# A token fold of 21 products with repeated operands, and row transposes in 128x128 blocks, in a fused attention and Fourier-mix kernel

## The chip, the cores and the metric

The kernel runs on one NeuronCore of a Trainium2 chip. The metric is the device time of one execution in microseconds (us); three executions of the kernel before gave a median of 248.39 us (248.08 to 248.51). The engines are named as in the profile: PE (matrix products; PEld is its weight load), DVE, ACT and POOL (vector, activation and general engines), SP (here a DMA issuer).

## The reference

```python
def reference(q, k, v, n_global, n_local, w_ch1, w_ch2):      # q, k, v: (4, 8, 768, 64) float32
    scores = q @ k.T / sqrt(64) - slope[h] * dist              # kept: causal band of 96, and the first 8 keys
    a = softmax(where(keep, scores, -1e9)) @ v
    x = a.transpose(0, 2, 1, 3).reshape(4, 768, 512)
    u = x + real(fft(fft(x, axis=1), axis=2))                  # over tokens, then over features
    un = (u - mean(u)) / sqrt(var(u) + 1e-6)
    return u + maximum(un @ w_ch1, 0) @ w_ch2                  # w_ch1: 512x2048, w_ch2: 2048x512
```

## The kernel before

The four batches go through four stages. **Attention**: q and k are loaded as fp16 and turned with the head dimension on the partitions (tile `pt`, copied to `qkT`), scores go to PSUM tiles `sc`, ACT takes the exponential (`ex`), and `av` (line 808) multiplies by v (tile `pav`) and normalises on DVE into `x`. In batch 0 and 1 the global keys come in through small copies `kB` and `vB` that POOL or DVE make. **Token fold**: the 768 tokens are six blocks of 128, and the six-point part of the transform over tokens combines them into six sums `z`. In batch 0 two of the four pairs of heads are folded on DVE and two (`PEF = (1, 3)`) on PE, by `fold_pe` (line 1004): each of the six sums is a chain of four or six 128x128 products of a scaled identity (1, -1, 1/2 or -1/2) with one block of `x`, 32 in all, into PSUM tile `pf`; ACT or DVE copies the result to `zy`. **Mix**: units `py` (line 1092; tables `t` over tokens), `px` (line 1156) and `pu` (line 1180; tables over features) add up to the rows `u`. **Feed-forward**: rows are centred into `un`, turned into `unT`, multiplied by the first matrix (`ph`, line 1329, 128 products of 256 columns for a chunk of 256 rows), passed through relu into `hT`, and multiplied by the second one (`pg`, or for later chunks a seven-product scheme with tiles `pgA` and `pgD`).

There are twelve chunks of 256 rows. The first three (`NTD = 3`) are turned by PE in `nt_unit` (line 1296): each of 2 x 4 blocks of 128x128 is cut into four 64x64 quarters, 32 transposes in all, each on its own quarter of the PE array, into the two PSUM banks of tile `ptu`; one copy by DVE (line 1321) or ACT (line 1319) brings it to `unT`. Later chunks are turned by DMA.

The order of work on each engine is a table written by hand, `Plan.ORDER` (line 242), of unit names for PE and of operation names for the others. A cost model of times in the class `Plan` walks that table: it only decides in which sequence the engines' lists are interleaved when the program is recorded, and which of several equal PSUM banks a unit takes. The recorded sequence in turn decides who waits for whom where two engines write parts of one tile.

Of the kernel before, what the change touches and what calls it, by code (L numbers as in the profile page):

```python
# [14 lines left out]
P = 128  # L15
# [9 lines left out]
class Plan:  # L25
# [9 lines left out]
    MIX = 1.3  # L35
    LANDED = {"HW": 0.55, "SW": 1.3}
    LAT = {"ACT": 0.14, "DVE": 0.12, "POOL": 0.08}
# [84 lines left out]
    def op_go(self, eng, name, start):  # L122
# [6 lines left out]
        if eng == "POOL":  # L129
            self.ports.append((start, end, 1 if dma else 0 if outs and outs[0][0] in ("vB", "kB") else 2))  # L130
        if dma:
            at = max(max(end + 0.55, 5.5) if eng == "POOL" else end + lat + 2.7 * (lat == 1.0 and end > 3.5), self.now)
# [19 lines left out]

    SHARED = {"kB": 1, "vB": 1, "sid": 1, "f1": 0, "f2": 0, "f3": 0, "z": 0, "g0": 0, "w": 0, "s": 0, "w2a": 0, "w2t": 0, "ex": 0}
# [3 lines left out]
    def beside(self, start, cost, kind):  # L157
# [4 lines left out]
        if names:  # L162
            s = self.op_start("POOL", names[-1])
            if s is not None:
                p = self.made[names[-1]]
                ports = ports + [(max(s, start), max(s, start) + p[0]["POOL"][0], 1 if p[7] else 0 if p[3] and p[3][0][0] in ("vB", "kB") else 2)]
# [15 lines left out]
    def move(self, go=False):  # L182
# [4 lines left out]
        both = [h[2] for k, h in act if k != "AQ" or sw]  # L187
        each = sum(both) * (self.MIX if len(both) > 1 else 1.0) / 1000.0
        rate = {k: h[2] / 1000.0 if k == "AQ" and not sw else each for k, h in act}
        t = min([self.now + h[1] * rate[k] for k, h in act] + [h[0] for k, h in heads if h[0] > self.now + 1e-9] + [self.NEVER])  # L190
        if not go:
            return t
# [3 lines left out]
        for k, q in self.q.items():  # L196
            if q and q[0][1] <= 1e-4:
                _, _, _, outs, uses, cell = q.pop(0)
                cell[0] = t + (1.3 + 0.4 * (t > 12) if k == "SW" else 1.1 if t < 8 else self.LANDED["HW"] + 0.7)
# [144 lines left out]
def act(n):  # L344
    return 0.1 + n / 1180.0
# [10 lines left out]
def pool(n):  # L356
    return 0.16 + n / 1080.0


@with_exitstack  # L360
def kernel(
# [156 lines left out]
    def load_v(b, hp):  # L518
        h0 = 2 * hp
        if b >= FB:  # L520
# [3 lines left out]
            swq(whole, 1.08, [("avdone", b - 2), ("wl", 7)], [("v", b, hp, t) for t in range(2)], (1536, 0.93), False)  # L524
            return
        if b == 1:
            for t in range(2 - hp % 2 * 2):
# [3 lines left out]
                swq(four, 1.08, [], [("v", b, hp, t), ("v", b, hp + 1, t)], (1536, 0.93))  # L531
            return
        for t in range(2):
# [3 lines left out]
            swq(run, 0.85, ([("avdone", b - 2), ("wl", 7)] if b > 1 else []), [("v", b, hp, t)], (768, 0.93), b < 2)  # L537
# [4 lines left out]
    def load_qk(b, hp):  # L542
# [3 lines left out]
        for w, src in enumerate((q, k)):  # L546
            if b >= FB:
                for h in range(2):
# [4 lines left out]
                    swq(run, 0.85, free(tag, ti) + [("wl", 7)], [("qk", n, w, h)], (768, 0.93), False)  # L553
# [25 lines left out]
            if n == 4:  # L579
# [5 lines left out]
                swq(two, 1.08, free(tag, ti), [("qk", n, w), ("qk", n + 1, w)], (1536, 1.53))  # L585
# [7 lines left out]
            swq(run, 0.85, free(tag, ti), [("qk", n, w)], (768, 1.53))  # L593
# [110 lines left out]
    def score(b, hp, g):  # L704
# [3 lines left out]
        def run(start, ring):  # L708
# [37 lines left out]
            e = pl.pe((0.45, 0.45, 0.34)[g] if pem else 0.24, start, "64x64" if pem else "64x32")  # L746
# [61 lines left out]
    def av(b, hp):  # L808
# [28 lines left out]
        def part(start, ring, x, k):  # L837
# [15 lines left out]
            pl.later([("DVE", 0.17 + 0.03 * m + m * dve(384), lambda: norm(po, k))], free(*XT[b]), e,  # L853
# [10 lines left out]
    def bounce(b):  # L864
# [26 lines left out]
        pl.later([("POOL", 1.1, rg)], xw + [("xr", b), ("c", "back")], 0.0, [("xg", b)], dma=(128, 4.94), rank=0)  # L891

    def fold_s(b):
# [3 lines left out]
        for n, (c0, cw) in enumerate(parts):  # L897
# [43 lines left out]
            pl.later([("DVE", (4 if b else 2) * dve2(cw), f3)], [("f2", b, n)], 0.0, [("f3", b, n)])  # L941
# [8 lines left out]
    def fold_0():  # L950
# [41 lines left out]
        def g0(x):  # L992
            if x == 0:
# [6 lines left out]
        ZS = (((one, 0), (one, 3), (one, 1), (one, 4), (one, 2), (one, 5)), ((one, 0), (neg, 3), (neg, 1), (one, 4), (one, 2), (neg, 5)),  # L1000
              ((one, 0), (one, 3), (mhlf, 1), (mhlf, 4), (mhlf, 2), (mhlf, 5)), ((one, 0), (neg, 3), (half, 1), (mhlf, 4), (mhlf, 2), (half, 5)),
              ((one, 1), (one, 4), (neg, 2), (neg, 5)), ((one, 1), (neg, 4), (one, 2), (neg, 5)))

        def fold_pe(hp):
            cols = slice(hp * P, (hp + 1) * P)

            def run(start, ring):
                zy()
                pf = bank(ring, f"pf_{hp}")
                for n, terms in enumerate(ZS):  # L1010
                    o = pf[:, n // 4, (n % 4) * P:(n % 4 + 1) * P]
                    for x, (w, i) in enumerate(terms):
                        nc.tensor.matmul(o, w, X[0][:, i, cols], start=(x == 0), stop=(x == len(terms) - 1))
# [120 lines left out]
    def mirror(b):  # L1134
# [8 lines left out]
        pl.later([("POOL", 0.8, lambda: r0(nc.gpsimd.tensor_copy)), ("DVE", 0.3, lambda: r0(V.tensor_copy))], [("y", b, 0, 3), ("y", b, 3, 3)] + free("rev0", b), 0.0,  # L1143
# [116 lines left out]
    def centre(c):  # L1260
# [11 lines left out]
        for a in range(2):  # L1272
            pl.later([("ACT", 0.62, lambda a=a: un("ACT", a)), ("DVE", 1.3 if c < 2 else 0.38, lambda a=a: un("DVE", a))],
# [13 lines left out]
        pl.later([("POOL", 0.82, rstd)], [("ss", c, 0), ("ss", c, 1)], 0.0, [("rstd", c)], rank=2)  # L1287
# [8 lines left out]
    def nt_unit(b, pr):  # L1296
# [4 lines left out]
        def run(start, ring):  # L1301
            pt = bank(ring, f"ptu_{c}", FP16)
            un = T.pop(("un", c))
            for a in range(2):
                for d in range(ND):
                    for i in range(2):
                        for h in range(2):
                            r, o, x = slice(64 * i, 64 * i + 64), d * P + 64 * h, 64 * (a * ND + d)
                            nc.tensor.transpose(pt[64 * h:64 * h + 64, i, x:x + 64], un[r, a, o:o + 64], idn[r, r],
                                                tile_position=(64 * i, 64 * h))  # L1310
# [40 lines left out]
    def store_back(c, needs):  # L1351
# [6 lines left out]
        pl.later([("POOL", 1.1, st)], needs, 0.0, [], [("free", "u", c + pl.U0)] * 2, dma=(128, 11.25), rank=0)  # L1358
# [71 lines left out]
    def s_sums(c):  # L1430
# [16 lines left out]
        def s1():  # L1447
            VT(new(0), block(1, 0), block(1, 1), op=ALU.add)

        def s3():  # L1450
            VT(block(1, 0), block(0, 0), block(1, 0), op=ALU.subtract)

        def s2():
            VT(new(1), SX[c, 0], block(0, 0), op=ALU.subtract)

        def s4():
            if lean:
                SX[c, 2] = SX[c, 1]
                VT(SX[c, 2], block(0, 1), SX[c, 1], op=ALU.subtract)
            else:  # L1460
                VT(new(2), block(0, 1), SX[c, 1], op=ALU.subtract)
        us = dve2(NK * P)

# [6 lines left out]
        pl.later([("DVE", us, s1)], hs + sfree(0), 0.0, [("s", c, 1)], rank=1)  # L1470
        pl.later([("DVE", us, s2)], [("s", c, 1)] + sfree(1), 0.0, [("s", c, 2)], [] if lean else [("free", "sx", k)], rank=1)
        pl.later([("DVE", us, s4)], [("s", c, 2)] + ([("p6", c)] if lean else sfree(2)), 0.0, [("s", c, 4)], [] if lean else [("free", "sx", k + 1)], rank=1)
        pl.later([("DVE", us, s3)], [("s", c, 1)], 0.0, [("s", c, 3)], rank=1)

# [132 lines left out]
    def dma_const(dst, src, us, tok, needs=(), soon=False):  # L1607
# [3 lines left out]
        pl.later(ways if soon else ways[:1], needs, 0.0, [tok], lat=1.0 if soon else 3.2, dma=us)  # L1611

    with tc.manual_schedule():
# [19 lines left out]
        swq(px, 0.62, [], [("c", "px")], (128, 3.0))  # L1633
        swq(lambda: table(0, nc.gpsimd), 0.66, [], [("c", "t1", 0)], (128, 7.5))
# [154 lines left out]
```

## Time and profile before

| | |
|---|---|
| Median of three executions | 248.39 us (248.08 to 248.51) |
| Profiled execution, its own time | 245.87 us |
| Its span, first to last instruction | 244.1 us |
| Mean granted PE clock | 0.991 |
| PE busy | 232.0 us, 95% of the span |
| DVE, ACT, POOL busy | 193.4, 138.8, 114.8 us |
| `pf`: two units of 32 products | first starts at 27.6 us, last at 32.7 us |
| `ptu`: three units of 32 transposes | first starts at 47.0 us, last at 63.9 us |

A row of the timeline gives the start, the duration, the engine, the line, the operation with its output and inputs, the size, and the count of merged instructions; an idle time before it stands in brackets with what ended it ("issue" where the profile shows nothing). A row of the chain of work gives the start of a stretch, its length, and the work. A row of a table by stretches gives the stretch, its length, and for each engine the busy time with the count of instructions in brackets.

### The profile page before, as it was taken

How to read it: one execution, taken by the hardware profiler on the slowest of the kernel's cores; microseconds unless marked ns; L12 is line 12 of the kernel's file. 1: busy time of each engine (PE TensorE's matmuls, PEld its weight loads, DVE VectorE, ACT ScalarE, POOL GpSimd, SP SyncE). 2: the span in 40 equal slices, each digit the busy share in tenths (PEclk: the TensorE clock that was granted, in tenths of full speed). 3: DMA queues.
4: the chain of work that ended last, by engine and by line, in shares of the span. 5: the costliest groups of instructions: out<-in, count | busy, mean ns of one | idle time of the engine just before them, and what ended most of it. 6: DMA issues, size and time to landing. Idle time of an engine off the chain costs nothing.

```text
span 244.1 us, 7606 instructions
## 1 busy us (share of the span) xinstructions
PE 232.0 (95%) x3251; PEld 191.2 (78%) x3251; DVE 193.4 (79%) x420; ACT 138.8 (57%) x226; POOL 114.8 (47%) x164
## 2 busy tenths in 40 slices
PE   7679899999999999999999999999999999999993
PEld 2557776878677667788989888898889898888883
DVE  2559997879972789999999889889998755846483
ACT  2368788864657468658357788364534651434200
POOL 8998898866590038999059056500300320011020
PEclk9997999999999999999999999999999999999999
DMA  6999999999999999999999979220570330040212
GB/s 170 181 169 145 157 235 172 197 190 196 110 145 152 234 179 205 117 135 110 242 184 285 135 84 156 46 33 13 174 258 4 77 99 0 1 130 1 89 72 99
DMA packets 95938, 32.85 MB, mean 135 GB/s; under 512 B 84160, under 2 KB 92480, under 8 KB 95904
## 3 DMA queue, kind: packets, MB, share of 16 engines
q0 software_dynamic: 66176, 17.06, 71.7%
q1 hardware_dynamic: 26560, 12.56, 25.1%
q10 hardware_dynamic: 3168, 2.75, 4.1%
q8 instruction: 25, 0.41, 0.7%
q14 instruction: 9, 0.07, 0.1%
HBM read 31.44 MB, written 8.65 MB: 164 GB/s over the span
## 4 chain that ended last, share of the span: by engine, by line
PE 67%; DMA 14%; DVE 5%; ACT 5%; POOL 3%; issue 3%; SPq 1%; POOLq 0%
PE ph L1339 29%; PE pgD L1484 14%; PE pgA L1484 10%; DMA qk<-in_q_dram 4%; DMA v<-in_v_dram 4%; PE py L1105 3%; DMA hT<-in_q_dram 3%; PE pg L1370 3%; PE pav L822 3%; ACT ex L766 2%; DMA back<-backm 2%; DMA xr<-xd,back 2%; PE sc L737 2%; PE pu L1192 1%; ACT mk L1657 1%
## 5 line engine op out<-in xcount | busy, mean ns | idle before, releaser
L1339 PE MATMUL ph<-unT,w 128*128 128x256 f16 x768 | 94.4, 273 | 0.8 <-issue 0.4
L1339 PEld LDWEIGHTS <-w 128*128 128x128 f16 x768 | 73.6, 98 | 12.5 <-issue 1.2
L1344 ACT ACTIVATE hT<-ph 128x512 f16<-128x512 f32 x73 | 42.9, 596 | 54.6 <-PE ph L1339 52.6
L1484 PEld LDWEIGHTS <-hT 128*128 128x128 f16 x320 | 31.0, 98 | 4.3 <-issue 0.4
L1285 POOL TENSOR_SCALAR sm<-sm 128x2 f32<-128x2 f32 x12 | 3.4, 284 | 58.2 <-ACT un L1278 57.8
L763 ACT ACTIVATE er<-sc 128x1024 f16<-128x1024 f32 (+1 forms) x24 | 22.3, 951 | 11.4 <-PE sc L737 8.2
L1345 DVE TENSOR_SCALAR hT<-ph 128x512 f16<-128x512 f32 x23 | 15.7, 687 | 12.7 <-PE ph L1339 12.7
L766 ACT ACTIVATE ex<-sc 128x1024 f16<-128x1024 f32 (+1 forms) x24 | 21.7, 955 | 7.1 <-PE sc L743 6.9
L1502 DVE SCALAR_TENSOR_TENSOR u<-pgA,sm,u 128x256 f32<-128x256 f32 (+1 forms) x30 | 16.9, 568 | 6.4 <-PE pgA L1484 6.0
L1502 DVE SCALAR_TENSOR_TENSOR u<-pgD,sm,u 128x512 f32<-128x512 f32 (+1 forms) x21 | 15.2, 722 | 3.5 <-PE pgD L1484 3.3
L1355 POOL DMA_INDIRECT out_dram<-u,back x4 | 4.5, 1120 | 27.5 <-DVE rev L1140 16.3
L887 POOL DMA_INDIRECT xr<-xd,back x3 | 4.8, 1602 | 25.4 <-PE pg L1370 16.1
L1370 PE MATMUL pg<-w,hT 128*128 128x512 f16 x64 | 16.0, 379 | 0.0
L1118 ACT ACTIVATE zy<-py 128x1024 f16<-128x1024 f32 (+1 forms) x13 | 11.1, 857 | 8.4 <-PE py L1105 6.1
L778 DVE TENSOR_TENSOR ex<-er,mk 128x1024 f16<-128x1024 f16 (+1 forms) x24 | 15.1, 646 | 0.7 <-ACT er L763 0.7
L1278 ACT ACTIVATE un<-un 128x512 f16<-128x512 f16 x24 | 15.0, 625 | 1.1 <-DMA unT<-un 1.1
L552 POOL DMA_DIRECT2D qk<-in_k_dram x16 | 13.7, 903 | 1.2 <-DMA w<-in_moe_w_ch_dram 0.8
L1269 ACT ACTIVATE un<-u,sm 128x512 f16<-128x512 f32 x19 | 13.1, 717 | 1.9 <-DVE sm L1251 0.7
L552 POOL DMA_DIRECT2D qk<-in_q_dram x16 | 13.6, 870 | 0.0
L822 PEld LDWEIGHTS <-ex 128*128 128x128 f16 x352 | 12.4, 97 | 1.1 <-ACT ex L766 0.4
L834 DVE TENSOR_TENSOR x<-pav,rc 128x384 f16<-128x384 f32 x24 | 12.6, 554 | 0.6
L822 PE MATMUL pav<-v,ex 128*128 128x65 f16 x224 | 12.9, 193 | 0.2
(170 smaller groups left out, 492.9 us busy)
## 6 DMA issues: line engine op xcount, KB each, us to landing
w<-in_moe_w_ch_dram POOLq DMA_DIRECT2D x8, 512.0 KB, 13.4
out_dram<-u SPq DMA_DIRECT2D x15, 256.0 KB, 3.0
v<-in_v_dram POOLq DMA_DIRECT2D x12, 192.0 KB, 5.8
qk<-in_k_dram POOLq DMA_DIRECT2D x16, 96.0 KB, 5.4
qk<-in_q_dram POOLq DMA_DIRECT2D x16, 96.0 KB, 4.5
xr<-xd SPq DMA_DIRECT2D x3, 512.0 KB, 4.6
xd<-x ACTq DMA_DIRECT2D x2, 768.0 KB, 4.5
v<-in_v_dram POOLq DMA_DIRECT2D x8, 96.0 KB, 7.0
```

The lines of the kernel that those rows point to most:

```text
L552: nc.gpsimd.dma_start(qk16[n][:, w, :, h], src[b, h0 + h].rearrange("(i m) d -> m i d", m=P))
L763: A(mine(), cut(pa), AF.Exp, 0.0, 0.125)
L766: A(cut(expst[hp][:, :, g * 512:g * 512 + (384 if g == 2 else 512)]), cut(pa), AF.Exp, 0.0, 0.125)
L778: VT(o, mine(), m, op=ALU.mult)
L822: nc.tensor.matmul(o[:, s * 65:(s + 1) * 65], lhsT, w, start=(a == 0), stop=(a == len(ops) - 1), skip_group_check=True)
L1278: A(x, x, AF.Square, accum_out=MV[c][:, a, 2:3])
L1339: nc.tensor.matmul(ph[:, a * CH:(a + 1) * CH].rearrange("p (x m) -> p x m", x=2), W1[0][:, d, jb * P:(jb + 1) * P], UNT[c][:, :, d, :], st ...
L1344: pl.later([("ACT", act(512), lambda: A(dst, ph, AF.Relu)), ("DVE", dve(512), lambda: V.tensor_scalar_max(dst, ph, 0.0))], [], e, [("h", c ...
L1345: ("DVE", dve(512), lambda: V.tensor_scalar_max(dst, ph, 0.0))],
L1370: nc.tensor.matmul(pg, HT[c][:, jb, t * P:(t + 1) * P], W2[0][:, jb, :], start=(jb == 0), stop=(jb == NJ - 1))
L1484: nc.tensor.matmul(o, lhs(j), rhs(j), start=(first and j == 0), stop=(j == NK - 1), skip_group_check=True)
L1502: V.scalar_tensor_tensor(o, x, r(t), acc, op0=ALU.mult, op1=ALU.add)
```

## The change

`fold_pe` orders its terms by operand, not by output. A term (`w, i, n, k, step`) multiplies block `i` of `x`, repeated `k` times along the columns, by one scaled identity, and adds it to `k` of the six sums at once; so 32 products of 128 columns become 21: one of 512, eight of 256 and twelve of 128 columns, which are 32 x 128 columns as before. `nt_unit` makes 8 transposes of 128x128 in place of 32 of 64x64, and writes all of them to one PSUM bank, which the copy reads in one piece.

Many constants of the cost model change as well (durations, DMA landing times, port sharing), one constant load may by the model go out on two queues, and the sums `s_sums` may by the model run on POOL for some chunks. The table `ORDER` is the same word for word, and it names neither of the two in another place, so both stay where they were. What the new constants do change is the interleaving: eight units swap between two equal PSUM banks, and in one place two copies that wait for each other change their order.

```diff
-        ZS = (((one, 0), (one, 3), (one, 1), (one, 4), (one, 2), (one, 5)), ((one, 0), (neg, 3), (neg, 1), (one, 4), (one, 2), (neg, 5)),
-              ((one, 0), (one, 3), (mhlf, 1), (mhlf, 4), (mhlf, 2), (mhlf, 5)), ((one, 0), (neg, 3), (half, 1), (mhlf, 4), (mhlf, 2), (half, 5)),
-              ((one, 1), (one, 4), (neg, 2), (neg, 5)), ((one, 1), (neg, 4), (one, 2), (neg, 5)))
+        ZT = ((one, 0, 0, 4, 1), (one, 3, 0, 2, 2), (neg, 3, 1, 2, 2), (one, 4, 0, 2, 1), (mhlf, 4, 2, 2, 1), (one, 2, 0, 2, 1), (mhlf, 2, 2, 2, 1),
+              (one, 1, 0, 1, 1), (neg, 1, 1, 1, 1), (mhlf, 1, 2, 1, 1), (half, 1, 3, 1, 1), (one, 5, 0, 1, 1), (neg, 5, 1, 1, 1), (mhlf, 5, 2, 1, 1), (half, 5, 3, 1, 1),
+              (one, 1, 4, 2, 1), (neg, 5, 4, 2, 1), (one, 4, 4, 1, 1), (neg, 4, 5, 1, 1), (neg, 2, 4, 1, 1), (one, 2, 5, 1, 1))
...
-                for n, terms in enumerate(ZS):
-                    o = pf[:, n // 4, (n % 4) * P:(n % 4 + 1) * P]
-                    for x, (w, i) in enumerate(terms):
-                        nc.tensor.matmul(o, w, X[0][:, i, cols], start=(x == 0), stop=(x == len(terms) - 1))
+                for x, (w, i, n, k, step) in enumerate(ZT):
+                    o = pf[:, n // 4].rearrange("p (n m) -> p n m", m=P)[:, n % 4:n % 4 + (k - 1) * step + 1:step]
+                    nc.tensor.matmul(o, w, X[0][:, i, cols].unsqueeze(1).to_broadcast([P, k, P]), start=i == 0 or (i == 1 and n == 4),
+                                     stop=(x in (len(ZT) - 1, 14)), skip_group_check=True)
...
-                    for i in range(2):
-                        for h in range(2):
-                            r, o, x = slice(64 * i, 64 * i + 64), d * P + 64 * h, 64 * (a * ND + d)
-                            nc.tensor.transpose(pt[64 * h:64 * h + 64, i, x:x + 64], un[r, a, o:o + 64], idn[r, r],
-                                                tile_position=(64 * i, 64 * h))
-            e = pl.pe(0.27, start, "64x64")
-            ptv = pt[:, :, 0:512].rearrange("p i (y m) -> p i y m", m=64)
+                    nc.tensor.transpose(pt[:, 0, (a * ND + d) * P:(a * ND + d + 1) * P], un[:, a, d * P:(d + 1) * P], idn)
+            e = pl.pe(0.46, start)
+            ptv = pt[:, 0]
...
-                o = t.rearrange("p a d (i m) -> p i (a d) m", i=2)
+                o = t.rearrange("p a d m -> p (a d m)")
...
-    LAT = {"ACT": 0.14, "DVE": 0.12, "POOL": 0.08}
+    LAT = {"ACT": 0.18, "DVE": 0.12, "POOL": 0.08}
...
-    return 0.1 + n / 1180.0
+    return 0.055 + n / 1180.0
```

On PE, the first fold unit follows a score unit (`sc`). It begins with these rows before; the weights are the identity (`ident`) or a scaled one (`misc`, `hid`), and brackets name the semaphores that a row waits for:

```order
L743 MATMUL sc_1_690<-qkT_623,mk 64x128
L1013 LDWEIGHTS ident [waits DVE_49]
L1013 MATMUL pf_716<-x_383,ident 128x128 [waits PE_49]
L1013 LDWEIGHTS ident
L1013 MATMUL pf_716<-x_383,ident 128x128
```

In the change the same place on PE reads:

```order
L753 MATMUL sc_1_692<-qkT_623,mk 64x128
L1022 LDWEIGHTS ident [waits DVE_49]
L1022 MATMUL pf_718<-x_383,ident 128x512 [waits PE_49]
L1022 LDWEIGHTS ident
L1022 MATMUL pf_718<-x_383,ident 128x2x128
L1022 LDWEIGHTS misc
L1022 MATMUL pf_718<-x_383,misc 128x2x128
```

Nothing moved around it; 11 weight loads and 11 products are gone from each of the two units. With 24 of each gone from each of the three transposing units, 188 of 6504 rows are gone from PE's list, and all that follow stand that much earlier in its instruction stream.

The third transposing unit on PE follows a unit of the first matrix product (`ph`). It begins so before:

```order
L1339 MATMUL ph_5_1606<-unT_1304,w_0_904 128x256
L1309 LDWEIGHTS un_1530 [waits DVE_49]
L1309 MATMUL ptu_1621<-ident,un_1530 64x64 [waits DVE_49]
L1309 LDWEIGHTS un_1530
L1309 MATMUL ptu_1621<-ident,un_1530 64x64
```

and so in the change:

```order
L1345 MATMUL ph_5_1536<-unT_1258,w_0_881 128x256
L1316 LDWEIGHTS un_1460 [waits DVE_49]
L1316 MATMUL ptu_1551<-ident,un_1460 128x128 [waits DVE_49]
L1316 LDWEIGHTS un_1460
L1316 MATMUL ptu_1551<-ident,un_1460 128x128
```

The units around it, `ph` before and `pg` (products of 512 columns) behind, are the same, and so are the waits. The shape on the array is now that of these neighbours.

On DVE, the copies of the mix units `py` to `zy` read before, with the semaphores that each waits for in brackets:

```order
L1120 CAST zy_1038<-py_0_998 128x512 [waits PE_49]
L1120 CAST zy_1038<-py_1_1058 128x512 [waits PE_49]
L1120 CAST zy_1038<-py_2_1073 128x512 [waits PE_49]
L1120 CAST zy_1038<-py_2_1073 128x512
L1215 SCALAR_TENSOR_TENSOR u_948,sm_949<-pu_1105,u_948 128x512 [waits PE_49,Activation_49]
```

and in the change:

```order
L1130 CAST zy_1016<-py_0_976 128x512 [waits PE_49]
L1130 CAST zy_1016<-py_1_1038 128x512 [waits Activation_49]
L1130 CAST zy_1016<-py_2_1051 128x512 [waits PE_49]
L1130 CAST zy_1016<-py_2_1051 128x512
L1225 SCALAR_TENSOR_TENSOR u_909,sm_910<-pu_1083,u_909 128x512 [waits PE_49]
```

The order is the same; the wait of the second row moved. Two halves of `py_1` are copied, one by DVE (this row) and one by ACT (its row 37). Before, ACT's half waited for DVE's; now DVE's half waits for ACT's.

More of the change, by code (lines that the diff above doesn't have):

```diff
@@ L129, in op_go @@
         if eng == "POOL":
-            self.ports.append((start, end, 1 if dma else 0 if outs and outs[0][0] in ("vB", "kB") else 2))
+            self.ports.append((start, end, 1 if dma else 0 if outs and outs[0][0] in ("vB", "kB", "ts", "w1s", "s") else 2))
         if dma:
-            at = max(max(end + 0.55, 5.5) if eng == "POOL" else end + lat + 2.7 * (lat == 1.0 and end > 3.5), self.now)
+            at = max(max(end + 0.95, 5.33) if eng == "POOL" else end + lat + 2.7 * (lat == 1.0 and end > 3.5), self.now)
             cell = [self.NEVER]
@@ L190, in move @@
         t = min([self.now + h[1] * rate[k] for k, h in act] + [h[0] for k, h in heads if h[0] > self.now + 1e-9] + [self.NEVER])
+        if sw and nxt > self.now + 1e-9:
+            t = min(t, nxt)
         if not go:
```

80 lines of the change are left out of this document (44 added, 36 removed).

## The prediction

> **What bounds the kernel now.** First the page: the span, each engine's share, and the queue that fetches instructions.
>
> ```profile
> span 244.1 us, 7606 instructions
> PE 232.0 (95%) x3251; PEld 191.2 (78%) x3251; DVE 193.4 (79%) x420; ACT 138.8 (57%) x226; POOL 114.8 (47%) x164
> q8 instruction: 25, 0.41, 0.7%
> ```
>
> PE is busy for 95%, so I asked where the rest lies, with a table by stretches (length, then PE, PEld, DVE, ACT, POOL busy).
>
> ```profile
> 0.00:54.35 54.35, 46.87 (x1023) 34.72 (x1023) 40.13 (x102) 37.49 (x52) 47.06 (x78) 0.97 1.66 179
> 54.35:94.30 39.95, 39.61 (x440) 28.28 (x441) 31.03 (x65) 24.79 (x42) 17.82 (x22) 1.00 1.42 172
> 94.30:105.00 10.70, 10.08 (x175) 8.19 (x175) 10.53 (x24) 7.98 (x14) 10.70 (x14) 1.00 1.67 148
> 105.00:240.40 135.40, 135.40 (x1614) 120.03 (x1613) 111.25 (x231) 68.51 (x121) 39.18 (x53) 1.00 0.61 105
> ```
>
> From 54.35 us on PE idles for 0.34 + 0.62 + 0 us; before it, for 7.5 us. So work taken from PE after 54.35 comes off the end almost one for one, and work taken before counts only if the point at 54.35 moves. The chain of work says what that point hangs on:
>
> ```profile
> 52.31 0.67 DVE vB L795
> 53.28 1.03 DVE tt L834 x2
> 54.36 0.84 PE pav L822 x22
> ```
>
> PE's `pav` waits for DVE's normalising of the `pav` before, which stands in DVE's list behind the copies `vB`, and these wait for a load of v. The timeline of DVE and POOL has that load, and its line's landing times (shortest, median, longest):
>
> ```profile
> 36.48 1.00 POOL L529 DMA_DIRECT2D v<-in_v_dram  x1
> 51.37 0.30 DVE L793 COPY vB<-v 128x528 f16<-128x528 f16 x1 [1.34 <-DMA v<-in_v_dram]
> DMA to landing us min/median/max: 9.2/10.2/14.8
> ```
>
> Issued at 36.48, landed 14.8 us later behind three weight loads: a queue of bytes, which no edit touches. DVE idles 1.34 us ahead of it, so DVE too is reset there. I call 54.36 **the pin**.
>
> **The change part by part.** What one product costs when they follow each other is in the chain: 40 of 256 columns, 16 of 128, 4 of 512.
>
> ```profile
> 220.06 4.37 PE ph L1339 x40
> 154.66 0.89 PE pu L1192 x16
> 58.49 0.86 PE pg L1370 x4
> L1013 PE MATMUL pf<-x,ident x32: 219/219/230, 27.6 to 32.6; 128*128 128x128 f16 x32
> ```
>
> That is 0.1093, 0.0556 and 0.215 us. **Fold**: before, 32 x 0.0556 = 1.78 us a unit; after, 0.215 + 8 x 0.1093 + 12 x 0.0556 = 1.76. The columns are the same, so 11 products fewer save 0.02 us, twice, between 27.6 and 32.7 us, ahead of the pin: nothing at the end. A repeated operand is known here from the score units, whose bias products take 512 columns plain in some and 256 twice in others, all at one line:
>
> ```profile
> L729 PE MATMUL sc<-misc x96: 322/388/631, 10.3 to 46.4; 64*64 64x512 f16 x64, 64*64 64x384 f16 x32
> ```
>
> The row gives no sign of two speeds at full clock. Bounds: at best nothing more; at worst the nine wide products run at half speed, 9 products of together 20 blocks, 20 x 0.0556 = 1.1 us a unit. I take no penalty, and 2.2 us for both would use up the slack at the pin that I work out below.
>
> **Transposes.** The third unit stands in the full stretch:
>
> ```profile
> 61.96 1.75 PE ph L1339 x16
> 63.71 0.38 PE ptu L1309 x32
> 64.08 2.69 PE pg L1370 x12
> ```
>
> From 63.71 to 66.78 are 3.06 us; twelve `pg` need 12 x 0.215 = 2.58, so the unit with its two changes of array shape costs 0.48. Eight products of 128 columns at 0.0556 are 0.445 with no change of shape: **-0.04 us**. The first unit follows a score unit of the same 64x64 shape, so it paid one change and will pay one, at its other side:
>
> ```profile
> 47.02 0.47 PE L1309 MATMUL ptu<-ident,un 64*64 64x64 f16 x32
> 47.42 0.28 PE L1192 MATMUL pu<-t,zy 128*128 128x128 f16 x2
> ```
>
> 0.40 us before, about 0.09 (the change of shape) + 0.445 after: +0.14, ahead of the pin. The second:
>
> ```profile
> 53.50 0.39 PE L1339 MATMUL ph<-unT,w 128*128 128x256 f16 x2 [0.38 <-issue]
> 53.83 0.45 PE L1309 MATMUL ptu<-ident,un 64*64 64x64 f16 x32
> 54.36 0.39 PE L822 MATMUL pav<-v,ex 128*128 128x65 f16 x7
> ```
>
> It ends about where it did, and PE waits there anyway. One change of shape is the difference of the two units, 0.48 - 0.40 = 0.08, called 0.09 above with what surrounds it. The copies out of `ptu`, now in one piece, gain nothing:
>
> ```profile
> L1319 ACT ACTIVATE unT<-ptu x2: 1019/1021/1023, 54.3 to 64.2; 128x1024 f16<-128x1024 f16 x2
> ```
>
> 1024 columns in pieces of 64 took ACT 1.02 us, as long as the 1024 of an exponential (its row, L766, is below), so the pieces cost nothing that could go.
>
> **Instruction blocks.** Two idle times of PE stand inside a unit with no releaser, at 41.0 (0.56) and 53.5 (0.38); a longer one, 1.53, at 15.8. Counted from each to the next:
>
> ```profile
> 0.00:17.30 17.30, 12.28 (x223) 1.00 1.53 173
> 17.30:41.00 23.70, 21.77 (x510) 0.93 1.84 175
> 41.00:53.45 12.45, 12.05 (x256) 1.00 1.49 194
> 33.76:41.00 7.24, 6.37 (x134) 1.00 2.71 184
> 47.00:53.45 6.45, 6.12 (x128) 1.00 1.67 185
> PE py L1105 <- issue: 0.6, 1, 0.6
> PE pt L652 <- issue: 1.5, 1, 1.5
> ```
>
> 510 and 256 products, with as many weight loads, are 1020 and 512 instructions; queue q8 brought 0.41 MB in 25 packets for 6502, so a packet holds 256. I read the stalls as blocks of 256 that land late. The 44 fewer instructions of the folds, and 48 of the first transposes, move these borders later: from 41.0 to about 41.4 (inside the next score unit) and from 53.5 past 56, where PE takes over 8 us for a block. So 0.38 us of stall goes, and the 0.56 is there again or not. The two blocks that were late came 7.24 and 6.45 us after the border before theirs (the last two rows of the stretches, of about 128 products each); the block between them was there in 6.0. The new borders leave about 6.4 us at 41.4 and 6.5 at the one behind it, so a stall there is between 0 and 0.9, and between 0 and 0.8. [...]
>
> **The moved wait.** Before, DVE copied its half of `py_1` first:
>
> ```profile
> 39.92 1.02 ACT L766 ACTIVATE ex<-sc 128x1024 f16<-128x1024 f32 x1
> 40.19 0.69 DVE L1120 CAST zy<-py 128x512 f16<-128x512 f32 x1 [0.86 <-PE py L1105]
> 40.92 0.60 ACT L1118 ACTIVATE zy<-py 128x512 f16<-128x512 f32 x1
> 41.64 1.29 DVE L1120 CAST zy<-py 128x512 f16<-128x512 f32 x2 [0.76 <-PE py L1105]
> 42.10 1.07 PE L1192 MATMUL pu<-t,zy 128*128 128x128 f16 x16
> ```
>
> ACT's half cannot start before its own exponential ends, 40.92; so DVE's now starts at 41.5 and ends at 42.2. Behind it DVE's next two copies slip from 41.64 to 42.2, and PE's `pu`, which reads both halves, from 42.10 to about 42.3: +0.2 on PE, +0.6 on DVE, which DVE pays back in its 1.34 us idle at 51.37. The bank swaps I cost at nothing: the units concerned run in the stretches from 94 and 105 us, where PE idles for 0.62 and 0 us in all, so the banks were empty when needed; if one of the eight were not, it would cost a part of the 0.6 us of one copy.
>
> **At the pin.** PE's transposes end near 54.1 and the change of shape near 54.2, so PE would be ready 0.15 us ahead of 54.36, and without the stall at 53.5 near 53.8: 0.5 us of slack. Against it stand +0.14 and +0.2, and the stalls at 41 (-0.56 to +0.35, beside what was there) and 48 (0 to +0.8): from nothing late to 1.0 late. I take it as covered: at -0.1 and +0.2, near the middle of both, the costs are 0.44 against 0.5. **Sum**: 245.87 - 0.04 = 245.83 by the profiled execution; the median of the runs lies 2.52 above that execution's time, so 248.35.
>
> **Rivals.** *Late at the pin.* Both moved borders stall at their upper bound; then 0.14 + 0.2 + 0.35 + 0.8 - 0.5 = 1.0 us reach `pav` at 54.36 and, with PE full behind it, the end: 249.3. It decides once these stalls together pass 0.5 us. For it: both borders leave less than the longest landing seen, 7.24. Against: the other two, 6.45 and 6.0, would do. *The pin is soft.* If PE's stalls of 0.56 and 0.38 had held back the end after all (PE is 97% busy from 41 to 53), they come off: 248.39 - 0.94 - 0.04 = 247.4. Against it: DVE's 1.34 us wait for v. *Wide or turned products do not overlap.* If each 128x128 transpose took its full 0.219 us (the duration of the `pf` row), a unit would cost 1.75 for 0.48, three units 3.8, less 0.5 of slack: 251.7. Against it: 24 transposes of 128 columns, two at a time, take 0.86 us here:
>
> ```profile
> 29.47 0.86 PE L652 MATMUL pt<-ident,qk 128*64 128x128 f16 x24
> ```
>
> [...]
>
> **How the numbers follow.** Forecast 0.66, late at the pin 0.16, soft pin 0.15, no overlap 0.03 (wide products at half speed, 2.2 us against 0.5 of slack, would end near 250 and are counted here). About 0.2% (0.5 us) is what a measurement of this kernel tells from no change; the three runs lie 0.4 us apart. The forecast's own range is 247.9 to 248.8; with the stalls' upper bound, 249.3, and half of the soft pin, the range is 247.8 to 249.3, and some 0.15 is left out. Faster by over 0.2% 0.15, within 0.66, slower 0.19.
>
> **What would show it.** Right: fold units of 1.76 us; the third `ptu` 0.445 long without gaps beside it; `pav` still released by DVE near 54.4; idle "issue" times of PE moved by 11 to 46 products. Wrong: that `pav` waits for nothing and starts later; the load of v lands at another time; or PE gains idle time behind 55 us, where I see no reason for any.

## The result, and the profile after

The changed kernel takes 251.07 us (median of 20 runs, 247.64 to 253.96), the kernel before 247.75 us in the same comparison (20 runs, 245.62 to 249.37): **1.08% slower, ratio 1.0108, 95% interval 1.0079 to 1.0137**. The forecast, 248.35 with a range to 249.3, was too low. Ratios here compare undisturbed runs alone (12 of the 20 of the changed kernel), the medians hold all of them and lie 1.3% apart. The profiled execution after took 250.15 us, 4.28 us more than the one before; that pair shows more than the ratio in part because the profiled execution before was a quick one (245.87, against a median of 247.75).

The page after, as far as its lines answer to those of before; the last row is POOL's gather of `xr` (an indirect DMA), with the idle time ahead of it and what ended most of that:

```profile
span 248.4 us, 7416 instructions
PE 232.6 (94%) x3157; PEld 191.0 (77%) x3157; DVE 195.0 (78%) x420; ACT 138.3 (56%) x226; POOL 114.2 (46%) x164
q8 instruction: 24, 0.39, 0.6%
L897 POOL DMA_INDIRECT xr<-xd,back x3 | 3.6, 1204 | 27.8 <-DMA back<-backm 18.5
```

PE's busy time is almost what it was (232.0 before), so most of the 4.3 us of span, 3.7, is idle time. The table by stretches of the changed kernel says where (length, then PE, PEld, DVE, ACT, POOL busy):

```profile
0.00:54.62 54.62, 46.70 (x959) 34.49 (x960) 40.55 (x102) 37.20 (x51) 47.02 (x78) 1.00 1.75 180
54.62:90.30 35.68, 35.68 (x368) 25.22 (x365) 26.18 (x54) 19.76 (x34) 13.54 (x17) 1.00 1.43 163
90.30:109.52 19.22, 15.22 (x236) 12.01 (x236) 16.75 (x37) 13.76 (x23) 17.58 (x22) 1.00 1.41 145
109.52:244.60 135.08, 134.91 (x1607) 119.31 (x1603) 110.99 (x229) 67.62 (x119) 36.02 (x49) 1.00 0.57 103
```

The same 236 products stand in the kernel before in this stretch, which ends at the end of the same unit of `pgA`:

```profile
90.30:105.94 15.64, 14.69 (x236) 11.92 (x234) 15.02 (x34) 12.67 (x21) 14.51 (x19) 1.00 1.53 155
```

At 90.30 both kernels are at the same product; 3.58 of the 4.28 us arise in this one stretch, 19.22 for 15.64. PE idles there for 4.00 us and not 0.95. Another 0.53 us is busy time (15.22 for 14.69), which I read as overlap of neighbouring products lost at the breaks (an estimate: a product of 128 columns has a row of 0.219 us, and in a sequence starts 0.0556 us behind the one ahead of it). The rest, 0.7 us, is spread over the 135 us behind.

So what the prediction called the wrong outcome came: PE gains idle time behind 55 us. Who ended the longest waits between 90 and 110 us, changed kernel first, kernel before second:

```profile
PE sc L747 <- DVE u L1258: 1.0, 1, 1.0
PE ph L1345 <- ACT hT L1350: 0.9, 1, 0.9
PE pgD L1493 <- DVE eg L1454: 0.7, 1, 0.7
PE sc L747 <- ACT er L773: 0.6, 1, 0.6
```

```profile
PE ph L1339 <- DMA unT<-un: 0.4, 1, 0.4
PE pgA L1484 <- DVE u L1502: 0.3, 1, 0.3
PE sc L737 <- ACT er L763: 0.2, 1, 0.2
```

DVE is late because two reads are late: the plain read `xr<-xd`, then POOL's gather `xr<-xd,back`. DVE's first instruction on each, before:

```profile
87.17 0.69 DVE L1232 SCALAR_TENSOR_TENSOR u<-pu,xr 128x512 f32<-128x512 f32 x1 [0.83 <-PE sc L737]
...
92.95 0.87 DVE L1244 SCALAR_TENSOR_TENSOR u<-pu,xr 128x384 f32<-128x384 f32 x1 [0.41 <-DMA xr<-xd,back]
```

and after, 1.24 and 3.05 us later:

```profile
88.41 0.69 DVE L1242 SCALAR_TENSOR_TENSOR u<-pu,xr 128x512 f32<-128x512 f32 x1 [2.02 <-DMA xr<-xd]
...
96.00 0.86 DVE L1254 SCALAR_TENSOR_TENSOR u<-pu,xr 128x384 f32<-128x384 f32 x1 [2.23 <-DMA xr<-xd,back]
```

ACT is late through DVE: its `un`, ahead of the `hT` that PE waits for, waits for DVE's `sm`. Before and after:

```profile
88.73 0.72 ACT L1269 ACTIVATE un<-u,sm 128x512 f16<-128x512 f32 x1 [0.49 <-DVE sm L1236]
...
89.96 0.72 ACT L1279 ACTIVATE un<-u,sm 128x512 f16<-128x512 f32 x1 [1.67 <-DVE sm L1246]
```

The gather needs the list `back`, a load of 2 KB that SP issues. SP's timeline, before and after (start, length, queue and line); then the gather's row on POOL after, and the landing time of `back`, before and after:

```profile
73.04 7.10 SPq L631 DMA_TRANSPOSE qkT<-qk  x3
...
83.26 0.42 SPq L1608 DMA_DIRECT2D back<-backm  x1
```

```profile
74.35 6.50 SPq L641 DMA_TRANSPOSE qkT<-qk  x3
...
83.97 0.44 SPq L1617 DMA_DIRECT2D back<-backm  x1
```

```profile
91.45 1.27 POOL L897 DMA_INDIRECT xr<-xd,back  x1 [18.46 <-DMA back<-backm]
```

```profile
DMA to landing us min/median/max: 4.8/4.8/4.8
```

```profile
DMA to landing us min/median/max: 6.6/6.6/6.6
```

Two delays: SP's transposes begin 1.3 us late, because the qk that they read lands late, and SP's later DMAs slip by 0.7 us; and `back` takes 6.6 us for 4.8. What falls on both loads in the changed kernel, and not before, is a block of PE's instructions. The row of queue q8 between 71.8 and 73.1 us, and between 87.8 and 88.9 (packets, MB, share of the 16 DMA engines):

```profile
q8 instruction: 1, 0.02, 5.6%
```

```profile
q8 instruction: 1, 0.02, 5.5%
```

5.6% of 16 engines for 1.3 us is one engine for 1.16 us: one packet of 16 KB. In the kernel before these blocks load at 63.88, 75.12 and 88.28; with 188 rows taken out of PE's list, each border is reached later, and the loads stand at 71.89 and 87.89.

For the qk load the landing records show the collision: it lands in 16 parts, and in the kernel before 15 are in by 72.53 us and the last at 72.90; in the changed kernel 15 are in by 72.89 and the last at 74.20, after the block (71.89 to 73.04). SP's transposes begin 0.15 us behind that. The records of the single packets show the collision at `back`, whose 2 KB are 128 packets of 16 bytes:

```
              issue   packets 1 to 120   packets 121 to 128   block of PE's instructions
before        83.26   86.41 to 87.42     87.42 to 87.44       88.28 to 89.33
changed       83.97   87.07 to 88.08     89.85 to 89.89       87.89 to 88.85
```

120 packets go through as before; the last 8, one sixteenth, start only after the block. The same holds for SP's write of 128 packets ahead of `back`: 120 by 87.95 us, 8 from 88.84 to 89.76. Eight of 128 packets, one part of sixteen of qk, and a record of 16 KB that takes one engine of sixteen for 1.16 us: I read from these numbers that one DMA engine is taken up by the record while its share of the other transfers waits. That is an estimate; the records here do not name the engine.

### The profile page after: what moved, and what is told of

Read it like the earlier page. It is cut to its first block, busy times and chain, and to the rows that moved or that the text cites. A ratio compares the mean times of both kernels' runs of the same rounds, so it can differ in the third digit from the quotient of the medians.

```text
span 248.4 us, 7416 instructions
## 1 busy us (share of the span) xinstructions
PE 232.6 (94%) x3157; PEld 191.0 (77%) x3157; DVE 195.0 (78%) x420; ACT 138.3 (56%) x226; POOL 114.2 (46%) x164
## 4 chain that ended last, share of the span: by engine, by line
PE 60%; DMA 19%; DVE 12%; POOL 3%; issue 2%; ACT 2%; SPq 0%; POOLq 0%; DVEq 0%; ACTq 0%
PE ph L1345 27%; PE pgD L1493 12%; PE pgA L1493 9%; DMA w<-in_moe_w_ch_dram 6%; PE pg L1376 3%; DMA hT<-in_q_dram 3%; PE pav L832 3%; DMA tt<-in_k_dram 3%; DMA back<-backm 3%; DMA out_dram<-u 2%; PE py L1115 2%; DMA xr<-xd,back 2%; DVE ex L788 2%; DVE u L1511 2%; ACT ex L776 1%
## 5 line engine op out<-in xcount | busy, mean ns | idle before, releaser
L1295 POOL TENSOR_SCALAR sm<-sm 128x2 f32<-128x2 f32 x12 | 4.0, 334 | 61.9 <-ACT un L1288 61.6
L788 DVE TENSOR_TENSOR ex<-er,mk 128x1024 f16<-128x1024 f16 (+1 forms) x24 | 16.4, 701 | 0.7 <-ACT er L773 0.7
L897 POOL DMA_INDIRECT xr<-xd,back x3 | 3.6, 1204 | 27.8 <-DMA back<-backm 18.5
```

Of the source, the lines that this page charges most:

```text
L788: VT(o, mine(), m, op=ALU.mult)
```

## The experiments

Each ran in five rounds against the kernel before; ratios are to it, with 95% intervals. The first four take the change apart: its moved waits and banks, its fold, its transposes, and the last two together.

**Moved waits and banks alone.** All constants of the planner's cost model as in the change, which move the wait of `py_1` and eight banks; fold and transposes as before.

```diff
-    LAT = {"ACT": 0.14, "DVE": 0.12, "POOL": 0.08}
+    LAT = {"ACT": 0.18, "DVE": 0.12, "POOL": 0.08}
...
-    return 0.1 + n / 1180.0
+    return 0.055 + n / 1180.0
```

> The kernel before with only the moved waits and the swapped banks of the change: DVE waits for ACT's half of the reduced py_1 instead of ACT for DVE's, eight units take another pair of banks; the fold keeps its 32 products and the transposes their 64x64 blocks. If the moved wait or a swapped bank is what costs (theory A), this is slower than before by the whole amount, 1.1% (2.6 us), with PE idle between 94 and 109 us of some 4 us in place of 1. If the products or the transposes themselves are the cause (theories B and D), it stays within 0.2% of before. If the cause is that a shorter PE program moves every later request and DMA (theory C), it stays within 0.2% too, since its PE program has as many instructions as before.

Measured: 247.45 us, ratio 0.9984 (0.9948 to 1.0019). Theory A falls.

**Fold alone.** The kernel before with the table and the loop of 21 products.

```diff
-                for n, terms in enumerate(ZS):
...
+                for x, (w, i, n, k, step) in enumerate(ZT):
```

> The kernel before with only the fold of 21 products (44 rows of PE fewer in all), and banks and waits as before. If products with repeated columns cost (theory D): slower than before by 1.1%, and the fold's products longer than their columns. If the order of waits (A) or the transposes (B) carry the result: within 0.2% of before. If any shift of the PE program does it (theory C: instruction blocks and the landing of the small load `back` fall otherwise): slower by 0.3 to 1.1%, with `back` landing later than 88.0 us.

Measured: 247.52 us, ratio 1.0004 (0.9976 to 1.0031). Theory D falls.

**Transposes alone.**

```diff
-                            nc.tensor.transpose(pt[64 * h:64 * h + 64, i, x:x + 64], un[r, a, o:o + 64], idn[r, r],
-                                                tile_position=(64 * i, 64 * h))
...
+                    nc.tensor.transpose(pt[:, 0, (a * ND + d) * P:(a * ND + d + 1) * P], un[:, a, d * P:(d + 1) * P], idn)
```

> The kernel before with only the transposes in 128x128 blocks (144 rows of PE fewer in all), and banks and waits as before. If the transposes are the cause (theory B): slower than before by 1.1%, PE idle between 94 and 109 us of some 4 us. If the order of waits (A) or the products (D) carry it: within 0.2%. If any shift of the PE program does it (theory C): slower by 0.3 to 1.1%, here and with the fold alone.

Measured: 248.18 us, ratio 1.0019 (0.9979 to 1.0058). Theory B falls. Theory C as I had put it, that any shift costs 0.3 to 1.1%, is in doubt: neither the shift by 44 rows nor this one, by 144, shows a cost, though the intervals just reach 0.3% and here 0.58%.

**Fold and transposes together**, with the two edits above.

> The kernel before with the fold of 21 products and the transposes in 128x128 blocks, but with the banks and waits of before: the change without its reordered waits. Theory A: within 0.2% of before. Theories B and D: slower by 1.1%, as the change itself. Theory C: slower by about 1%, and by more than either part alone unless they overlap.

Measured: 250.71 us, ratio 1.0123 (1.0069 to 1.0176). Two parts that cost nothing cost 1.2% together. What they share is the number of rows, 44 + 144 = 188, and this run's trace has the block loads and late reads of the changed kernel. That gave the theory of the blocks, which says that only the place of the borders counts, and the next runs move the borders without touching the work.

**Borders moved ahead of the changed kernel.** PE's warm-up is 15 products of 512 columns, from 1.45 to 6.19 us in the kernel before, ahead of PE's first product on an input (6.41); the first parts of an input land meanwhile, from 3.23. More and narrower ones, with the same columns in all, push every later row back.

```diff
-        for _ in range(pl.PZ):
-            nc.tensor.matmul(pz[:, 0, :], EG[:, 0, 0:P], EG[:, 0], start=True, stop=True)
+        for _ in range(37):
+            nc.tensor.matmul(pz[:, 0, 0:208], EG[:, 0, 0:P], EG[:, 0, 0:208], start=True, stop=True)
```

> The changed kernel with 22 more products in PE's warm-up (37 of 208 columns for 15 of 512: the same columns in all, before any input has landed), so 44 more rows in front of everything. Its block borders then lie where those of the kernel with the transposes alone lay. Block theory (PE's instructions come in blocks of 256 rows, one 16 KB packet each; in the changed kernel a block loads at 71.9 us, on the landing of the qk load that SP's second transpose after the pause waits for, and the next at 87.9, on xr and `back`): the block of 71.9 moves to about 66, SP's transpose starts about 1 us sooner against DVE's work, and the time falls to 247.5 to 248.3. Rival (two small savings together let PE run ahead into waits, or the wide products and turned blocks cost something together; blocks don't matter): it stays at 250.0 to 251.5.

Measured: 248.28 us, ratio 1.0011 (0.9974 to 1.0047). As the block theory has it.

**The kernel before, with the changed kernel's borders.** The same edit with 49 products of 157 columns.

> The kernel before, fold and transposes untouched, with 34 more products in PE's warm-up (49 of 157 columns for 15 of 512), 68 more rows in front of everything: 68 more and 188 fewer are the same place within a block of 256, so its borders lie where the changed kernel has them. Block theory: a block loads near 72 and one near 88, and the kernel before becomes as slow as the changed one, 250.0 to 251.2 (+0.8 to +1.4%). Rival: nothing of the change is in it, so within 0.2% of before, or slower by the longer warm-up at most (about 0.3 us).

Measured: 251.80 us, ratio 1.0153 (1.0093 to 1.0213). None of the change is in this kernel, and it is as slow. Its waits of PE between 90 and 110 us are those of the changed kernel:

```profile
PE ph L1339 <- ACT hT L1344: 1.0, 1, 1.0
PE sc L737 <- DVE u L1248: 0.7, 1, 0.7
PE pgD L1484 <- DVE eg L1448: 0.6, 1, 0.6
PE sc L737 <- ACT er L763: 0.6, 1, 0.6
```

and so are POOL's gather, and the landing of `back`:

```profile
92.71 1.29 POOL L887 DMA_INDIRECT xr<-xd,back  x1 [18.54 <-DMA back<-backm]
```

```profile
DMA to landing us min/median/max: 6.7/6.7/6.7
```

Of its 128 packets of `back`, 120 start between 88.24 and 89.21, the last 8 from 91.10; a block loads from 89.15 to 90.10.

**`back` issued early.** In SP's order T.10 is `back`, T.136 the transpose at 64 us, T.35 the load `distk`, T.91 the read of `xr`:

```diff
-            "T.6 T.0 T.9 T.136 T.35 T.127 T.133 T.128 G7.1 T.134 T.91 G3.1 T.10 T.137 T.130
+            "T.6 T.0 T.9 T.136 T.10 T.35 T.127 T.133 T.128 G7.1 T.134 T.91 G3.1 T.137 T.130
```

> The changed kernel with the 2 KB load `back` issued by SP some 20 us sooner, ahead of `distk` at 64 us, so that POOL's gather of xr no longer waits for it. If the lateness of `back` is what costs (POOL waited for it at 91.45, while xr had landed by 88.3): the gather goes at about 88.5 and the time falls by 1.5 to 2.5 us, to 248.5 to 249.5. If the later landing of qk and xr carries the loss by itself, and the gather is only a bystander: within 0.3 us of the changed kernel (250.5 to 251.2).

Measured: 248.85 us, ratio 1.0050 (1.0014 to 1.0085). Half of the loss goes, although the first block still delays qk. The gather goes at 81.8, and its transfer now runs beside the plain read of `xr`, on which DVE waits longer; in this trace a block takes 2.24 us there, from 85.24, and of the 16 parts of `xr` 15 are in by 88.31 and the last at 89.61. Which of the two delays `xr` is not shown.

> The kernel before with `back` issued some 20 us sooner, as in the run ahead. There xr had landed at 87.1 and the gather went at 88.94, at the landing of `back`: it can go 1.8 us sooner. PE had 0.95 us of idle time between 91 and 105 us that hangs on this chain. If that time goes: 246.6 to 247.2; if another wait ends it: 247.4 to 247.9.

Measured, the same edit on the kernel before: 247.96 us, ratio 1.0002 (0.9962 to 1.0042). Nothing is gained where the block did not hold `back` up. The gather goes at 83.3 here. In the kernel before the profile named a unit of PE, over at 88.09, as what released it; that unit cannot have been it, and `back`, in at 88.03, was.

**The changed kernel with the borders of before**, 109 warm-up products of 70 columns.

> The changed kernel with 94 more products in PE's warm-up (109 of 70 columns for 15 of 512): 188 more rows in front, as many as the change takes out, so the borders behind the third turned unit lie where the kernel before has them. Block theory: blocks load near 75 and 88.3 us against DVE's work, and the whole change then costs what was forecast for it, 247.4 to 248.3, with PE's idle time between 90 and 109 us back to about 1 us. Rival (the saved PE work itself does harm): 250 to 251.5.

Measured: 246.60 us, ratio 0.9970 (0.9938 to 1.0002), below the 247.4 to 248.3 that I had forecast, and the lowest ratio here. PE's stretch and its waits between 90 us and the same `pgA`, the gather, and the landing of `back`:

```profile
90.00:106.70 16.70, 15.92 (x251) 13.05 (x250) 16.02 (x36) 13.52 (x22) 15.49 (x20) 1.00 1.48 148
```

```profile
PE pgA L1493 <- DVE u L1511: 0.3, 1, 0.3
PE ph L1345 <- DMA unT<-un: 0.3, 1, 0.3
```

```profile
89.46 1.21 POOL L897 DMA_INDIRECT xr<-xd,back  x1 [15.88 <-PE pg L1376]
```

```profile
DMA to landing us min/median/max: 4.7/4.7/4.7
```

PE idles there for 16.70 - 15.92 = 0.78 us, and the whole change costs nothing.

**Two more positions**, the kernel before with 38 products of 202 columns and with 93 of 83.

> The kernel before with 23 more products in the warm-up (38 of 202 columns), 46 rows: borders between those of the changed kernel and those of before. Block theory: the loads move to about 73 and 88 us; the first is then past the landing that SP's transpose at 73 waits for, the second is still on the tail of xr and `back` or just past it: 248 to 250.5, and the trace must show the late `back` if it is slow and a `back` on time if it is not. Rival (a longer warm-up by itself costs, as in the run with 34): between 0 and +1.0%, in proportion to the products added, with blocks that fall on nothing.

Measured: 248.47 us, ratio 1.0048 (1.0013 to 1.0083). A block of 1.7 us falls on the qk load, so that SP's transposes are late, the next loads at 88.01, when all of `back` is through (87.39). By the ratio that is half the loss; the trace is of a run of 246.29 us, the quickest of the twelve, and shows the delays but not a typical time.

> The kernel before with 78 more products in the warm-up (93 of 83 columns), 156 rows, more than twice those of the slow run with 34. Block theory: loads near 64, 81 and 91 us, between the known fast positions: 247.2 to 248.5. Rival (a longer warm-up costs): slower than the run with 34, over 251.8.

Measured: 249.86 us, ratio 1.0081 (1.0043 to 1.0119). A miss, since I had forecast 247.2 to 248.5. SP and `back` are on time in its trace; a block loads during POOL's gather, and DVE gets it 0.8 us later; PE idles for 1.15 us at 97 us, of the 2.0 us that the ratio gives. That fits the theory, but was only seen afterwards, and does not account for the whole; nor is it the over 251.8 of the rival.

**`back` just ahead of `xr`** in SP's order of the changed kernel, two DMAs sooner.

```diff
-            "T.6 T.0 T.9 T.136 T.35 T.127 T.133 T.128 G7.1 T.134 T.91 G3.1 T.10 T.137 T.130
+            "T.6 T.0 T.9 T.136 T.35 T.127 T.133 T.128 G7.1 T.134 T.10 T.91 G3.1 T.137 T.130
```

> The changed kernel with `back` issued by SP directly ahead of xr in place of two DMAs behind it, so that it lands before the block of 87.9 us; the block of 71.8 and the 0.7 us by which SP is then late stay. If most of the loss comes from `back` behind the block (POOL's gather 2.5 us late, 1.8 of it there): 248.5 to 249.5, with the gather at 86 to 88 us and xr as late as in the changed kernel. If most comes from the later xr<-xd (DVE's u at 88.4 for 87.2 and PE's 0.92 us at 91.2): 250 to 251.

Measured: 248.54 us, ratio 1.0000 (0.9966 to 1.0033). By the ratio, two swapped DMAs take the loss away, with the work and the borders of the changed kernel. The single runs spread widely (245.62 to 252.05), and by the medians of all of them it is still 0.35% slower. The trace, of a run of 250.83 us, shows why: the gather goes on time, at 86.80, but now the plain read of `xr` meets the block (89.20 to 90.16). Of its 16 parts, 15 are in by 88.98 and the last at 91.20; DVE waits for it, and PE behind that:

```profile
91.33 0.69 DVE L1242 SCALAR_TENSOR_TENSOR u<-pu,xr 128x512 f32<-128x512 f32 x1 [3.67 <-DMA xr<-xd]
PE ph L1345 <- ACT hT L1350: 2.6, 1, 2.6
```

So the swap takes `back` out of the block's way and leaves `xr` in it.

**A whole block more.** The miss at 93 products left open whether a longer warm-up costs. 143 products of 54 columns are 256 rows more, one block, and leave every border where it was:

> The kernel before with 128 more products in the warm-up (143 of 54 columns, as many columns in all): 256 rows, exactly one block, so behind the warm-up every border lies where it lay. Block theory: 247.3 to 248.5, against the 251.8 of the run with only 34 more. Rival (a longer warm-up costs by its count): 252 or more.

Measured on the kernel before: 248.14 us, ratio 1.0003 (0.9961 to 1.0045). The trace, of a run of 249.94 us, shows more delay than that: a block takes 2.07 us from 76.49, DVE waits 1.4 and 1.1 us for the two reads of `xr`, and PE's waits between 90 and 112 us add up to 2.9 us, for 0.9 in the trace of before. So the same borders do not give every execution the same time.

> The changed kernel with one full block of 256 rows ahead of it: every border lies as in the changed kernel. Block theory: slow as the changed kernel, 250.2 to 251.8, although 94 more products made it fast. Rival (any longer warm-up of narrow products helps the changed kernel): 246.5 to 248.5.

Measured on the changed kernel: 251.01 us, ratio 1.0122 (1.0084 to 1.0159). By these times the fast one stays fast and the slow one slow: the length of the warm-up shows no cost, the place within a block does.

> The changed kernel with the 94 more products of the fastest run and `back` directly ahead of xr in SP's order. There the gather went at 88.8 against DVE's work, bound by `back`. If the 0.3 us of PE's idle time before ph at 95 us hang on the gather: 246.2 to 246.6. If the gather, started sooner, shares the DMA queues with xr and delays it (as where `back` was moved in the changed kernel alone: xr 1.6 us later): 246.8 to 248.0.

Measured, 109 warm-up products and `back` ahead of `xr`: 247.72 us, ratio 0.9982 (0.9946 to 1.0017). No gain over the 109 alone, as in the second case.

The traces on one clock: DVE's `misc<-w` (L1420, L1426 in the change) is set to its start before, 82.55 us, since executions stand up to 2 us apart by then. SP's transpose is the one at 73.04 of before; the column behind it has how long after the fifteenth part of its qk load the sixteenth landed. The four runs with `back` moved are left out.

```
kernel, rows ahead of it                   block loads    SP's transpose  16th part  gather   ratio
before                                0    75.1  88.3     73.0            0.37       88.9
before, 128 warm-up products          0    74.5  88.2     73.2            0.07       89.5     1.0003
waits and banks alone                 0    75.4  88.0     73.2            0.16       88.9     0.9984
changed, 94 warm-up products          0    74.9  88.2     73.1            0.06       88.8     0.9970
fold alone                          -44    77.8  88.8     73.0            0.01       89.1     1.0004
transposes alone                   -144    83.5  93.2     73.3            0.37       89.1     1.0019
changed, 22 warm-up products       -144    84.1  93.1     73.4            0.04       89.2     1.0011
before, 23 warm-up products         +46    72.3  88.8     75.4            1.61       89.7     1.0048
before, 78 warm-up products        +156    81.6  90.0     72.8            0.01       88.6     1.0081
fold and transposes                -188    71.6  87.9     74.0            0.93       91.4     1.0123
changed                            -188    71.8  87.8     74.3            1.31       91.4     1.0108
before, 34 warm-up products         +68    72.0  87.9     74.3            0.91       91.4     1.0153
changed, 128 warm-up products       +68    71.8  87.4     74.2            1.29       90.4     1.0122
```

Wherever a block loads near 72 us, one part of sixteen of the qk load is 0.9 to 1.6 us late, and nowhere else over 0.4.

## Why the prediction was wrong

**Fold: right.** 1.76 us a unit was forecast without a penalty for repeated operands. The first unit of the changed kernel, first and last row of PE's timeline:

```profile
26.91 0.50 PE L1022 MATMUL pf<-x,ident 128*128 128x512 f16 x2
...
28.62 0.22 PE L1022 MATMUL pf<-x,ident 128*128 128x128 f16 x1
```

28.62 + 0.0556 - 26.91 = 1.77 us.

**Transposes: right.** 0.445 us was forecast, with overlap. The chain of the changed kernel has the second and the third unit, and the pin:

```profile
54.17 0.45 PE ptu L1316 x8
54.62 0.67 PE pav L832 x22
...
63.79 0.45 PE ptu L1316 x8
```

**The pin: right in size, by luck.** `pav` starts 0.26 us late, within the 0 to 1.0 that I had worked out, but not by what I had added up. The unit of transposes now ends right ahead of it and PE no longer waits for DVE there: the sign that I had named, `pav` waiting for nothing and starting later, came. The stalls at 41.0 and 53.5 are gone, and PE waits elsewhere, for a weight load that it did not wait for before and that my working had no term for:

```profile
49.83 1.92 PE L1345 MATMUL ph<-unT,w 128*128 128x256 f16 x16 [1.04 <-DMA w<-in_moe_w_ch_dram]
```

Why that load is late was not followed. PE does not idle at all from the pin to 90.30, so neither the 1.0 us of *late at the pin* nor the saving of *soft pin* is what happened.

**The moved wait and the banks: right**, ratio 0.9984 by themselves.

**The instruction blocks: the step that failed.** I had the mechanism's first half: blocks of 256 rows, whose borders move when rows are taken out. I priced a border only by the stall of PE that fetches it, and let the blocks behind 53.5 us go with "where PE takes over 8 us for a block". In the changed kernel PE indeed never waited for those: behind 55 us its waits add up to 4.0 us, for 0.9 before, and each of them has a releaser. But other transfers came late where a block's packet loaded, the qk load by 1.3 us and `back` by 1.8, and as both were due at once, the engines that waited for them paid (DVE's first instructions on the two reads of `xr` stood 1.24 and 3.05 us later). The sum lacked this term: by the timed ratio 0.0108 x 247.75 = 2.7 us. I also took too narrow a view of what hangs on SP: `back`, a load of 2 KB and issued 5.7 us ahead of its use, left the gather no slack before, which the trace of before shows (gather at 88.94, `back` in at 88.03) and I did not look for, as no edit touched it. Two sizes were off besides. The 20 runs of the kernel before have a median of 247.75 and not 248.39, so the base was 0.6 us high and hid a part of the loss; and they spread over 3.75 us, so the 0.2% that I took from three runs as what a measurement can tell was too small.

How the loss divides between the two blocks is not settled. With only the first in the way the kernel before lost 0.5%; with `back` taken out of the second's way the changed kernel loses 0.5% or, by the other placing, between nothing and 0.35%. So by these times the block at 88 carries about half or more. That the 16 KB packet itself blocks one DMA engine rests on the timing of the 8 packets, on the one late part of sixteen of qk, and on the moved borders; a kernel that loads the same bytes at the same time without PE's blocks was not tried. The 0.7 us in the 135 us behind were not traced; they are gone in the run with 109 warm-up products, but also in the trace of fold and transposes together, which has the borders of the changed kernel, so the borders there do not explain them.

## What to carry to other kernels

The edit here changed the number of instructions, and with it more than the engine that executes them: with 188 rows fewer on PE its later instruction blocks loaded elsewhere (71.89 and 87.89 us, for 63.88, 75.12 and 88.28), and where in these runs a block met the qk load, `back` or the plain read of `xr` in flight, the last part of it came 0.9 to 2.2 us behind the rest. When a change that should be neutral is not, shift the borders with dummy instructions in an idle place (a part of a block, a whole block) before explaining the edit itself; here the time moved with the shift (ratio 1.0153 for the kernel before with 68 rows ahead) and returned after a whole block (1.0003 with 256), which says that the place of the borders is what cost. A small load that something waits for may be worth issuing ahead of the large ones: that took the loss here from 1.1% to 0.5% or less, though a block then met the next load that was due, `xr` (its last part 2.2 us behind the fifteenth).

## What the runs showed of the hardware

- PE's 6502 rows came in 25 packets of 16 KB before, its 6314 in 24 in the change, so about 256 rows a packet; one took 0.88 to 2.24 us (behind 20 us, in all traces).
- In the changed kernel, with such a packet from 87.89 to 88.85 us, 8 of the 128 packets of each of two DMAs on SP's queue came after it: 8 writes of 2048 bytes (88.84 to 89.76, the other 120 by 87.95), then 8 of `back` (89.85 to 89.89, the other 120 by 88.08), whose load landed 6.6 us after its issue for 4.8 before, 1.8 us more, for a packet of 0.96.
- The qk load that SP waits for lands in 16 parts. Where a block loads near 72 us, the sixteenth came 0.91 to 1.61 us after the fifteenth, elsewhere 0.01 to 0.37.
- Products with an operand repeated along columns, 512 and 256 columns wide, ran at the rate of plain ones: the unit of 21 products took 1.77 us for 1.76 by the columns.
- The number of products in PE's warm-up, from 15 to 143 with the same columns, showed no effect by itself (ratios 1.0003 on the kernel before, and 1.0122 for 1.0108 on the changed one).
